# Pooled attention into a Gelu MLP: values of attention two slots later, and the remainder's query loads split three and five

## The chip, the cores and the metric

The kernel runs on one core of a Trainium2 chip, in one launch. The metric is device time in microseconds (us). Before the change the median of seven runs is 279.15 us (278.59 to 280.13).

Five engines share the work: TensorE (PE, with its weight loads PEld), VectorE (DVE), ScalarE (ACT), GpSimd (POOL) and SyncE (SP, which here only issues DMAs). Sixteen DMA engines move data for all of them.

## The reference

Attention with keys and values that are averaged over eight neighbours, and then an MLP on its output:

```python
B, H, S, D = 8, 8, 576, 64
k_p = k.reshape(B, H, S // 8, 8, D).mean(axis=3)
v_p = v.reshape(B, H, S // 8, 8, D).mean(axis=3)
attn = softmax(q @ k_p.T / sqrt(D))          # 576 x 72 for each batch and head
x = (attn @ v_p).transpose(0, 2, 1, 3).reshape(4608, 512)
out = gelu_tanh(x @ w_in) @ w_out            # w_in 512 x 2048, w_out 2048 x 512
```

Inputs and output are float32; the kernel's matmuls take bf16.

## The kernel before, in words

**Tiling.** The 4608 rows are worked off in nine blocks of 512. Blocks 0 to 7 are the first 512 rows of each batch. The remaining 64 rows of all eight batches make the ninth block, R. The order is `seq` = 0, 1, ..., 6, R, 7. A step is one turn of the loop at L826; it is numbered here by its place in `seq`, so step 7 works on R. Each step has the MLP of its own block and, woven into it, the attention of the next block. In step 2, and from step 3 on in a `fast` form, this is so:

- The hidden layer, `hidden_fast` (L462): products of 128x256 tiles (L474) that save a multiplication in eight by sums and differences made on VectorE (`x_sums`, L448, recorded at L458), and ordinary products (L383). The partial results lie in two PSUM tiles, `x4` and `y4`. ScalarE and VectorE empty them in turn: L500, L502, L507, L510, L513, L517. ScalarE applies Gelu.
- The output layer in `mlp` (L536): seven products of 16 matmuls (L586), also with sums and differences.
- The attention of the next block: pooling on VectorE (L149, L151, L152, L165), transpose of the pooled keys by a DMA (L211, into `kTd`), their spread into `kbd` on GpSimd (L218, recorded at L94), spread of values on GpSimd (L172), scores (L248), exponentials (L257), sums and normalization (L264, L273, L279), transpose of the weights by four DMAs (L306, into `eT`), and the values (`values`, L326; matmuls at L344, for R at L355), whose result is copied to `xT` by three copies on ScalarE and one on VectorE (L361, recorded at L92 and L94). `xT` is what the next step's first products read.

**Order.** The order on each engine is written out by hand. TensorE's matmuls of a step have slot numbers: 0 to 63 for the hidden layer, 64 to 175 for the output layer (64 + 16 n + 8 p + m for product n, half p and matmul m). `at(hooks, s, f, ...)` (L771) puts the instructions of `f` ahead of the matmul of slot s on whatever engine they run. So the scores stand at slots 68 and 90, and the values at 64 + 104 (L892): between the two halves of the last product, with eight matmuls behind them before the next step begins. Step 1 splits the values in two, at 64 + 100 and 64 + 107 (L889, L890).

**Loads.** Loads and stores of blocks are issued by SP, those of R's queries by GpSimd. They are eight transfers of 128 KB, one for each batch (L125), which fill one tile `q_sb`. They are issued at slot 9 of the steps that lie three and two places ahead of R in the order: four in step 4 (batches 0 to 3) and four in step 5 (batches 4 to 7), in the loop at L896. Ahead of each group a tiny copy on GpSimd (`gate_queries`, L196) waits for L502 of the same step, so that the transfers don't start earlier. `load_q` takes a half-open range of columns, two batches to a column.

Of the kernel before, what the change touches and what calls it, by code (L numbers as in the profile page):

```python
# [19 lines left out]
def kernel(  # L20
# [21 lines left out]
    nc = tc.nc  # L42
    B, H, S, D = q.shape
# [9 lines left out]
    R = B  # L53
# [63 lines left out]
    def load_q(g, j0, j1, eng):  # L117
        t = st[g]["q"]
        if g < B:
            src = q[g, :, :MAIN, :].rearrange("h (p j) d -> p h j d", j=4)  # L120
            eng.dma_start(out=t[:, :, j0:j1], in_=src[:, :, j0:j1])
        else:
            for b in range(2 * j0, 2 * j1):
                p0 = 64 * (b % 2)
                eng.dma_start(out=t[p0:p0 + 64, :, b // 2, :], in_=q[b, :, MAIN:, :].rearrange("h t d -> t h d"))  # L125

# [518 lines left out]
    load_half(0, "k", nc.sync)  # L645
    load_half(0, "v", nc.sync)
    load_q(0, 0, 2, nc.sync)
    load_main(0, "v", 0, 2, nc.sync)
    load_main(0, "v", 2, 4, nc.sync)
    load_q(0, 2, 4, nc.sync)  # L650
    nc.scalar.preload_act_table_set(EXP_SET)

# [99 lines left out]
    load_half(1, "k", nc.sync)  # L752
    load_half(1, "v", nc.sync)
    load_q(1, 0, 4, nc.sync)
    for c in range(4):
        w_out_load(c)
# [14 lines left out]
    def at(hooks, s, f, *a):  # L771
        hooks.setdefault(s, []).append(lambda: f(*a))
# [6 lines left out]
    hooks = {}  # L779
# [46 lines left out]
    for n_, g in enumerate(seq):  # L826
        if n_ == 0:
            continue
        hooks = {}
        fast = n_ >= 3  # L830
        if n_ == 1:
            for i in range(1, 4):
                at(hooks, i, w_sums, i, 0, NP, nc.vector)
            at(hooks, 36, g_sums, 0, 4)
            at(hooks, 57, g_sums, 4, 6, (0,))
        elif fast:
            at(hooks, 41, g_sums, 0, 2, (0,))
            at(hooks, 57, g_sums, 2, 6, (0,))
            at(hooks, 65, g_sums, 6, 8, (0,))
            at(hooks, 65, g_sums, 0, 4, (1,))  # L840
        else:
            at(hooks, 20, g_sums, 0, 2)
            at(hooks, 36, g_sums, 2, 4)
            at(hooks, 57, g_sums, 4, 6, (0,))
        if not fast:
            at(hooks, 65, g_sums, 6, 8, (0,))
        at(hooks, 64 + 32, g_sums, 4, 8, (1,))
        if n_ + 1 < len(seq):
            n = seq[n_ + 1]
            b = B - 1 if n == R else n  # L850
            kv = n != B - 1
            if n_ == 1:
                for j in range(4):
                    at(hooks, 22 + 4 * j, cast_q, n, j, j + 1, nc.scalar)
                at(hooks, 35, qT_tile, n)
                at(hooks, 35, q_transpose_dma, n)
            if kv and not fast:
                t0 = 22 if n_ == 1 else 12
                at(hooks, t0, pool, b, 0, 5)
                at(hooks, t0, dup_k, b, 0, 5)  # L860
                at(hooks, t0, kT_tile, b, None)
                at(hooks, t0, k_transpose_dma, b)
                t1 = t0 + (16 if n_ == 1 else 24)
                at(hooks, t1, pool, b, 5, 9)
                at(hooks, t1, k_spread, b, [nc.gpsimd, nc.gpsimd])
                at(hooks, t1, spread_v, b, nc.gpsimd)
            elif kv:
                at(hooks, 5, pool, b, 0, 5, (0,))
                at(hooks, 17, pool, b, 0, 5, (1,))
                at(hooks, 17, dup_k, b, 0, 5)  # L870
                at(hooks, 17, kT_tile, b, None)
                at(hooks, 17, k_transpose_dma, b)
                at(hooks, 17, spread_gated, b)
                at(hooks, 40, k_spread, b, [nc.gpsimd, nc.gpsimd])
            if fast:
                at(hooks, 2, qT_tile, n)
                at(hooks, 2, q_transpose_dma, n)
            sc_at = [68, 68, 90, 90]
            for j in range(4):
                at(hooks, sc_at[j], scores, n, j)  # L880
                at(hooks, sc_at[j] + 1, exps, n, j)
            at(hooks, 80, eT_tile, n)
            for j in range(4):
                at(hooks, 80 if j < 2 else 92, norm, n, j, nc.vector if j > 1 else nc.gpsimd)
                at(hooks, 80 if j < 2 else 92, e_transpose_dma, n, j)
            at(hooks, 64 + 66, nc.scalar.preload_act_table_set, GELU_SET)
            at(hooks, 64 + 100, xT_tile, n)
            if n_ == 1:
                at(hooks, 64 + 100, values, n, (0,))  # L889
                at(hooks, 64 + 107, values, n, (1,))  # L890
            else:
                at(hooks, 64 + 104, values, n)  # L892
        if n_ + 2 < len(seq):
            n2 = seq[n_ + 2]
            s2 = 44 if n_ == 1 else 57
            for half, ahead in enumerate((3, 2)):  # L896
                if n_ + ahead < len(seq) and seq[n_ + ahead] == R:
                    if half == 0:
                        at(hooks, 9, q_tile, R)
                    at(hooks, 9, gate_queries, g)  # L900
                    at(hooks, 9, load_q, R, 2 * half, 2 * half + 2, nc.gpsimd)
            if n2 != R:
                at(hooks, s2, q_tile, n2)
                at(hooks, s2, load_q, n2, 0, 4, nc.sync)
            at(hooks, 64 + 52, cast_gated, n2)
            if n_ < 2:
                at(hooks, 64 + 100, qT_tile, n2)
                at(hooks, 64 + 100, q_transpose_dma, n2)
                at(hooks, 64 + 100, load_kv, n2, (1,))
            elif n2 != B - 1:  # L910
                b2 = B - 1 if n2 == R else n2
                at(hooks, 64 + 84, pool, b2, 5, 9, (0,))
                at(hooks, 64 + 97, pool, b2, 5, 9, (1,))
            if n_ == 1:
                at(hooks, 45, load_kv, n2, (0,))
            else:
                at(hooks, 28, load_kv, n2)
        mlp(g, hooks, n_ + 1 == len(seq), fast)
# [30 lines left out]
```

## Time and profile before

| What | us |
|---|---|
| median of 7 runs | 279.15 |
| lowest and highest | 278.59, 280.13 |
| the profiled execution | 279.03 |
| its span in the profile | 277.1 |
| TensorE busy | 269.1 (97%) |
| VectorE busy | 222.6 (80%) |
| ScalarE busy | 176.2 (64%) |
| GpSimd busy | 81.8 (30%) |
| bytes moved by DMA | 54.37 MB, 196 GB/s in the mean |

Times in the lines of a profile are counted from the start of the span. A line of a timeline has the start, the length, the engine, the line of the kernel, the operation with its tiles, and in brackets the idle time of the engine before it with what ended it. `x16` counts instructions. TensorE's granted clock is at full speed in all forty slices of the page. Landing of a DMA is counted from the start of its issue. "SPq" and "POOLq" are the queues of SP and GpSimd.

### The profile page before, as it was taken

The page shows a single profiled execution, that of the slowest core. Times are in us where ns is not written, and L with a number is a line of the kernel's source. Part 1 is how long each engine was busy: PE and PEld are TensorE (multiplying, and loading weights), DVE is VectorE, ACT ScalarE, POOL GpSimd, SP SyncE. Part 2 cuts the span into 40 slices and gives each one's busy share as a digit, 9 for nine tenths or more (in the row PEclk, how much of TensorE's full clock was granted, in tenths as well). Part 3 has the DMA queues.
Part 4 walks back from the last instruction along what each step waited for, and adds up shares of the span by engine and source line. Part 5 has one row for each costly group of instructions (what it writes and reads, how often), then busy time and mean ns, then how long its engine had stood idle before and what let it go on. Part 6 is the DMA issues. An engine that isn't in the chain of part 4 may idle for free.

```text
span 277.1 us, 6558 instructions
## 1 busy us (share of the span) xinstructions
PE 269.1 (97%) x2668; PEld 192.5 (69%) x2686; DVE 222.6 (80%) x365; ACT 176.2 (64%) x265; POOL 81.8 (30%) x122
## 2 busy tenths in 40 slices
PE   8989999999999999999999999999999999999995
PEld 3668844446854587668866876688668966886684
DVE  5887769999966798989999979899989558956832
ACT  1586576488546764696469636964796469656820
POOL 4740272006420544314264445433223300300000
PEclk9999999999999999999999999999999999999999
DMA  7999999998989895799399988974842460243013
GB/s 235 308 192 287 368 386 223 301 359 217 255 201 242 254 282 142 176 307 246 115 223 283 266 147 205 237 202 125 174 155 47 125 151 2 50 103 98 1 41 114
DMA packets 67856, 54.37 MB, mean 196 GB/s; under 512 B 41458, under 2 KB 53746, under 8 KB 67826
## 3 DMA queue, kind: packets, MB, share of 16 engines
q1 hardware_dynamic: 65186, 50.67, 70.2%
q0 software_dynamic: 2496, 3.15, 6.4%
q8 instruction: 21, 0.34, 0.5%
q10 hardware_dynamic: 144, 0.13, 0.1%
q14 instruction: 9, 0.07, 0.1%
HBM read 36.70 MB, written 9.44 MB: 166 GB/s over the span
## 4 chain that ended last, share of the span: by engine, by line
PE 85%; DVE 7%; DMA 4%; issue 1%; SPq 1%; ACT 1%; DVEq 0%
PE mm L586 28%; PE mm L383 22%; PE c L474 13%; PE mm L399 5%; PE mm L394 5%; PE xo L344 3%; PE x L586 3%; DMA eT<-eb 2%; DMA q_sb<-in_q_dram 2%; PE sc L248 2%; DVE den L264 1%; PE mm L531 1%; DVE eb L279 1%; ACT gT L490 1%; DVE eb L291 1%
## 5 line engine op out<-in xcount | busy, mean ns | idle before, releaser
L383 PE MATMUL mm<-xT,w_in_b 128*128 128x512 bf16 x290 | 68.1, 379 | 0.7
L586 PEld LDWEIGHTS <-gT 128*128 128x128 bf16 x512 | 48.3, 98 | 9.0 <-issue 1.4
L385 ACT ACTIVATE gT<-mm 128x512 bf16<-128x512 f32 x76 | 43.5, 599 | 15.3 <-PE mm L383 15.0
L383 PEld LDWEIGHTS <-w_in_b 128*128 128x128 bf16 x304 | 29.7, 98 | 30.8
L586 PEld LDWEIGHTS <-stage 128*128 128x128 bf16 x384 | 37.5, 98 | 4.4
L92 ACT CAST xT<-xo 128x512 bf16<-128x512 f32 (+1 forms) x24 | 13.2, 610 | 29.9 <-PE xo L344 25.4
L586 PE MATMUL mm<-tw,gT 128*128 128x256 bf16 x240 | 30.0, 273 | 0.0
L586 PE MATMUL mm<-w_out_b,gT 128*128 128x256 bf16 x240 | 29.9, 273 | 0.0
L279 POOL TENSOR_TENSOR eb<-e,r 128x576 bf16<-128x576 f32 x14 | 15.8, 1149 | 45.5 <-DVE r L273 24.8
L264 DVE TENSOR_REDUCE den<-e 128x8 f32<-128x576 f32 x36 | 26.2, 728 | 2.8 <-ACT e L257 2.8
L257 ACT ACTIVATE e<-sc 128x576 f32<-128x576 f32 x36 | 22.5, 650 | 7.8 <-POOL eb L279 5.9
L586 PE MATMUL mm<-tw,stage 128*128 128x256 bf16 x224 | 26.7, 273 | 0.0
L92 ACT COPY osb<-mm 128x512 f32<-128x512 f32 x30 | 17.8, 593 | 13.8 <-PE mm L586 13.2
L149 DVE TENSOR_TENSOR kv<-kv 128x1024 f32<-128x1024 f32 (+3 forms) x19 | 22.2, 1166 | 3.0 <-DMA kv<-in_k_dram 1.8
L172 POOL TENSOR_TENSOR vbd<-kvb,vmask 128x256 bf16<-128x256 bf16 (+2 forms) x38 | 21.8, 595 | 7.3 <-DVE kvb L152 6.4
L94 POOL CAST q_b<-q_sb 128x1024 bf16<-128x1024 f32 (+1 forms) x15 | 17.6, 1191 | 20.1 <-DMA q_sb<-in_q_dram 20.1
L474 PEld LDWEIGHTS <-ws 128*128 128x128 bf16 x192 | 18.8, 98 | 6.1 <-issue 0.2
L279 DVE TENSOR_TENSOR eb<-e,r 128x576 bf16<-128x576 f32 x18 | 17.8, 987 | 0.6
L474 PE MATMUL c<-tt,ws 128*128 128x256 bf16 x144 | 17.7, 272 | 0.0
L434 DVE TENSOR_TENSOR stage<-gT 128x512 bf16<-128x512 bf16 (+1 forms) x25 | 13.5, 541 | 4.2 <-ACT gT L385 2.3
L94 POOL COPY kbd<-kTd 64x288 bf16<-64x288 bf16 x12 | 6.5, 544 | 34.7 <-DMA kTd<-kvb 34.3
L435 DVE TENSOR_TENSOR gT<-gT 128x512 bf16<-128x512 bf16 (+1 forms) x25 | 13.2, 528 | 3.4 <-ACT gT L385 1.2
(107 smaller groups left out, 424.5 us busy)
## 6 DMA issues: line engine op xcount, KB each, us to landing
kv<-in_k_dram SPq DMA_DIRECT2D x7, 1024.0 KB, 7.3
q_sb<-in_q_dram SPq DMA_DIRECT2D x7, 1024.0 KB, 9.8
kv<-in_v_dram SPq DMA_DIRECT2D x6, 1024.0 KB, 9.4
out_dram<-osb SPq DMA_DIRECT2D x12, 512.0 KB, 3.0
out_dram<-osb SPq DMA_DIRECT2D x11, 256.0 KB, 3.3
kv<-in_v_dram SPq DMA_DIRECT2D x4, 512.0 KB, 10.1
w_in_b<-in_moe_w_in_dram POOLq DMA_DIRECT2D x4, 512.0 KB, 6.7
w_out_s<-in_moe_w_out_dram SPq DMA_DIRECT2D x2, 1024.0 KB, 13.7
```

Of the source, the lines that this page charges most:

```text
L92: eng.copy(out=out, in_=in_)
L94: eng.tensor_copy(out=out, in_=in_)
L149: add(out=t[:, :, 0:4, :], in0=t[:, :, 0:4, :], in1=t[:, :, 4:8, :], op=ALU.add)
L172: eng.tensor_tensor(out=vbd[p0:128, b, n0:n1, :].rearrange("p (c r) (hh d) -> p c (r hh) d", c=max(m, 1), d=D), in0=kvb[p0:128, 4 + c0:4 + ...
L257: nc.scalar.activation(out=e.rearrange("p (x h) s -> p x (h s)", x=2), in_=sc[:, :, 0:4 * Sp], func=ACT.Exp, scale=1.0 / 64.0)
L264: nc.vector.reduce_sum(out=den, in_=e, axis=AX.X)
L279: eng.tensor_tensor(out=o.rearrange("p (pr hh s) -> p hh pr s", hh=2, s=Sp), in0=e.rearrange("p (hh pr) s -> p hh pr s", hh=2), in1=r.rear ...
L383: nc.tensor.matmul(out=hp, lhsT=w_in_b[:, ko, fo * 128:(fo + 1) * 128], rhs=st[g]["xT"][:, ko, :], start=(i == 0), stop=(i == KO - 1))
L385: nc.scalar.activation(out=gT[:, fo, :], in_=hp, func=ACT.Gelu_apprx_tanh)
L394: nc.tensor.matmul(out=hp[:, f, :], lhsT=w_in_b[:, ko, (fo + f) * 128:(fo + f + 1) * 128], rhs=st[g]["xT"][:, ko, c0:c0 + 256], start=(ko ...
L474: nc.tensor.matmul(out=acc[:, m, :], lhsT=lhs(i, m), rhs=rhs(i), start=bool(fresh and i == 0 and m % 2 == 0), stop=(i == 1), skip_group_ch ...
L586: nc.tensor.matmul(out=xs[p] if acc is xs else acc[:, p, :], lhsT=lt, rhs=rt, start=bool(fresh and m == 0 and (p == 0 or (last and acc is ...
```

## The change

In steps 2 to 7 the values stand two slots later, at 64 + 106, so that six matmuls of the last product lie behind them and two more ahead. `load_q` for R takes a range of batches now, and the loop gives it batches 0 to 2 in step 4 and batches 3 to 7 in step 5. No instruction is added or removed.

```diff
-            for b in range(2 * j0, 2 * j1):
+            for b in range(j0, j1):
                 p0 = 64 * (b % 2)
                 eng.dma_start(out=t[p0:p0 + 64, :, b // 2, :], in_=q[b, :, MAIN:, :].rearrange("h t d -> t h d"))
...
             else:
-                at(hooks, 64 + 104, values, n)
+                at(hooks, 64 + 106, values, n)
...
-            for half, ahead in enumerate((3, 2)):
+            for ahead, b0, b1 in ((3, 0, 3), (2, 3, B)):
                 if n_ + ahead < len(seq) and seq[n_ + ahead] == R:
-                    if half == 0:
+                    if b0 == 0:
                         at(hooks, 9, q_tile, R)
                     at(hooks, 9, gate_queries, g)
-                    at(hooks, 9, load_q, R, 2 * half, 2 * half + 2, nc.gpsimd)
+                    at(hooks, 9, load_q, R, b0, b1, nc.gpsimd)
```

## The prediction

> Steps are numbered by their place in `seq`: step 2 works on batch 2, step 7 on the remainder R, step 8 is the last. A boundary is the stretch from the values of the next step (L344, L355) to its first product (L474).
>
> **What bounds the kernel now.** I read the page first, then the chain of waits, then the timelines of single engines at the places that the chain names, last the DMA queues there.
>
> ```profile
> PE 269.1 (97%) x2668; PEld 192.5 (69%) x2686; DVE 222.6 (80%) x365; ACT 176.2 (64%) x265; POOL 81.8 (30%) x122
> ```
>
> TensorE is busy for 97% of the span; only a place where it stands still can gain or lose time. The stretches from first product to first product (steps 3, 4, 5, 7) show how much stands still:
>
> ```profile
> 109.04:136.60 27.56, 27.45 (x297) 20.70 (x297) 25.28 (x40) 19.11 (x29) 8.27 (x13) 1.00 0.76 203
> 136.60:165.01 28.41, 27.66 (x296) 20.64 (x296) 25.57 (x41) 19.09 (x29) 13.05 (x18) 1.00 0.99 233
> 165.01:192.66 27.65, 27.54 (x296) 20.85 (x296) 25.49 (x40) 19.10 (x29) 11.69 (x18) 1.00 0.75 182
> 220.86:248.30 27.44, 27.34 (x296) 20.71 (x296) 20.11 (x34) 18.50 (x27) 2.26 (x2) 1.00 0.31 68
> ```
>
> The first number after the stretch is its length, the last but one the share of time in which the DMA engines work. Step 4 is 0.85 us longer than step 3 and its DMA engines never rest (0.99). The chain tells where the time lies (start, length, what):
>
> ```profile
> 104.58 2.63 DMA eT<-eb
> ...
> 107.26 0.97 PE xo L344 x24
> ...
> 117.03 1.85 PE c L474 x16
> ...
> 144.58 1.86 PE c L474 x16
> ...
> 159.21 3.98 DMA eT<-eb
> ...
> 163.22 0.97 PE xo L344 x24
> ...
> 173.00 1.84 PE c L474 x16
> ...
> 178.72 0.49 PE sc L248 x32
> ...
> 200.65 1.85 PE c L474 x16
> ...
> 228.84 1.75 PE c L474 x16
> ```
>
> Three kinds of stop. (a) The values wait for the fourth transpose of the weights (eT) in steps 2 and 4. In TensorE's timeline of step 4:
>
> ```profile
> 162.18 0.41 PE L344 MATMUL xo<-eT,vbd 32*64 32x256 bf16 x8
> 163.22 0.97 PE L344 MATMUL xo<-eT,vbd 32*64 32x256 bf16 x24 [0.64 <-DMA eT<-eb]
> ```
>
> The values run from 162.18 to 164.20, 2.02 us, against 1.19 us in step 3: 0.83 us lost. In step 2 they take 1.46 us: 0.27 us lost.
>
> (b) The last two products of the hidden layer (16 matmuls, L474) take 1.84 to 1.86 us in steps 3 to 6 and 1.75 us in steps 7 and 8. The 0.10 us is a wait for VectorE: the second of the two writes into the bank that L513 reads. VectorE in step 5:
>
> ```profile
> 165.63 0.42 DVE L458 TENSOR_TENSOR tt<-xT 128x512 bf16<-128x512 bf16 x1 [0.66 <-ACT xT L92]
> ...
> 171.18 1.21 DVE L510 COPY stage<-c 128x1024 f32<-128x1024 f32 x1
> 172.53 1.22 DVE L513 TENSOR_TENSOR stage<-c,stage 128x1024 f32<-128x1024 f32 x1
> ```
>
> From 165.63, when ScalarE's third copy of xT lets it start, VectorE has eleven instructions without a gap (the left-out lines have no bracket), L513 ends at 173.75, and the product starts at 173.80. So in steps 3 to 6 this chain of VectorE, which starts with the values, is the bound up to here. In step 7 there is no pooling in it and it waits for TensorE.
>
> (c) In step 5 the scores (0.49 us instead of 0.38) wait for the spread of k on GpSimd, which waits for the transpose of k:
>
> ```profile
> 177.46 1.25 POOL L94 COPY kbd<-kTd 64x288 bf16<-64x288 bf16 x2 [2.23 <-DMA kTd<-kvb]
> ```
>
> 177.46 + 1.25 = 178.71, and the second half of the scores starts at 178.76. Nothing is in hand there: R's queries are loaded just ahead of it.
>
> **The change part by part.**
>
> **Values two slots later**, in steps 2 to 7. No instruction is added. Eight matmuls after the values take 0.88 us (164.13 to 165.01), so two slots are 0.22 us. Before the values TensorE has 0.22 us more to do, after them six matmuls (0.66 us) instead of eight.
> - At a boundary that waits for eT (steps 2, 4) up to 0.22 us of the wait is filled and the next step's products start 0.22 us earlier.
> - At the others (3, 5, 6, 7) the values, the three copies of xT on ScalarE, the copy of x behind them (L611) and VectorE's chain come 0.22 us later, the first product does not. The first copy was done at 164.61 for a product at 165.01: 0.40 us in hand, 0.18 after; no wait. L611 frees the bank of hidden(0): it ended at 166.09 for a matmul at 166.76, still 0.45 in hand. But VectorE's chain has nothing in hand in steps 3 to 6: the product behind L513 comes 0.22 us later relative to the first product, whichever boundary lies before. That is 4 x 0.22 = 0.88 us, if nothing absorbs it. In steps 7 and 8 the product at 229.55 has 0.26 us over L513's end (229.29) and the chain there starts from TensorE: nothing.
>
> **Queries of R: three in step 4, five in step 5.** Eight issues of 0.71 us on GpSimd as before (L125), one of them in another step. In step 4 GpSimd is 0.71 us earlier with vbd; in step 5 it is 0.71 us later: vbd ended at 175.23 and the next, the spread of k, waited 2.23 us for its DMA, so this is hidden; without that cover it would cost the scores 0.71 us. SP's queue has no step moved past; but its loads queue behind the same engines.
>
> What one transfer costs the DMA engines, in step 5 (168.5 to 178.5), and then single microseconds from 174 and from 175:
>
> ```profile
> q0 software_dynamic: 192, 0.52, 25.3%
> ```
> ```profile
> q0 software_dynamic: 3, 0.01, 8.1%
> ```
> ```profile
> q0 software_dynamic: 47, 0.13, 81.7%
> ```
>
> 25.3% of 10 us is 2.53 us for four: 0.63 us each; in step 4 (140 to 150) the share is 21.2%, 0.53 us each.
> - Step 4: the engines are full from the loads to the transposes; the load of the next queries, issued at 147.31, lands 12.1 us later at 159.4, and the fourth eT, queued behind, at 163.18. One transfer less takes 0.53 us off; the loads are issued 0.22 us later, as VectorE's chain is. Estimate: 163.18 - 0.53 + 0.22 = 162.9. The bounds are 162.0 (issue at 159.4 and the 2.6 us of the uncrowded steps) and 163.4 (nothing gained).
> - Step 5: does the fifth transfer hold up the transpose of k? It was issued at 171.29 and landed 6.1 us later, against 2.6 us in steps 3 and 6, where no R is loaded. From below zero: a transfer ahead of it can't make it land earlier, so no gain. From above: all of 0.63 us. The row for the fourth transfer speaks for the low end: issued at 171.70, it has 3 packets on the engines in 174 to 175 and its 47 only in 175 to 176, when k's transpose is through; it landed after 5.5 us. A fifth, issued 0.7 us behind it, would follow. The Trainium skill speaks for the high end: "DMA: Bandwidth & Descriptors", section on queues, rings and completion order, says that each engine goes round-robin between the queues at packet level, so that what is issued on GpSimd takes turns with the transpose. By the row the cost is 0, by the rule up to 0.63. The two completions at 177.17 and 177.40 lie so close that I can't exclude some delay; I take 0.3 us, the middle.
>
> **The sum**, as shift of TensorE against before:
> - boundary 2: -0.22; behind L513 in step 3: +0.22, so 0.
> - behind L513 in step 4: +0.22.
> - boundary 4: the half that waits is now due at 162.59 + 0.22 + 0.22 = 163.03, eT lands at 162.9: no wait. Values end at 162.18 + 0.44 + 1.19 = 163.81 against 164.20, and the step starts 0.22 earlier still: -0.60.
> - behind L513 in step 5: +0.22, so -0.38; scores in step 5: +0.3, so -0.08.
> - behind L513 in step 6: +0.22. Total +0.14 us.
>
> The profiled execution took 279.03 us (span 277.1 and 1.9 around it), so 279.17; the median of the seven runs is 0.12 above it: 279.15 + 0.14 = 279.3.
>
> **The rivals.**
> 1. Slower: the fifth transfer holds up k's transpose in step 5 by its whole 0.63 us or more, the place with nothing in hand. For it: k's transpose lost 3.5 us (6.1 against 2.6) behind four transfers, 0.88 each; with 0.88 in place of 0.3 the sum is +0.72: 279.9. It decides from a delay of 0.72 us (sum +0.56) on. Against it: the order of the packets. Chance 0.22.
> 2. Slower by step 4: eT does not land earlier, because one engine of sixteen lags and not the sum of bytes. For it: the first two eT of step 4 landed 5.0 and 5.8 us after issue, and between 174 and 175 in step 5 the engines moved 25 GB/s while a transpose hung. eT at 163.4 instead of 162.9 puts 0.37 us plus 0.2 for the restart back (before, 0.64 us of waiting cost 0.83): +0.7, 279.85. Chance 0.13.
> 3. Faster: VectorE's chain gives way (a gap that the profile doesn't show, or TensorE catching up in a later wait), so the three lags in steps 4 to 6 are not paid. Then -0.22 - 0.83 + 0.3 = -0.75: 278.4. For it: both stops of kind (a) are what the edits touch; against it: the 0.10 us wait of kind (b) is in all four steps. Chance 0.15.
> The likeliest case, +0.14 with 0 to 0.63 us for the disputed term, has 0.50: 279.0 to 279.5.
>
> **How the numbers follow.** A measurement can tell about 0.2% from no change, 0.56 us: 278.6 to 279.7. Likeliest case: within. Rivals 1 and 2: slower. Rival 3: faster. So 0.15, 0.50, 0.35. The range takes in rival 3 to just above its value and rival 1 with some margin, leaving 0.2 out: 278.5 to 280.2.
>
> **What would show it.** Right: in the chain the eT entry at step 4's end is gone or under 0.2 us; the 16 matmuls of L474 take about 2.07 us in steps 3 to 6 and 1.75 in 7 and 8; step 5's spread of k starts up to 0.6 us later against its first product than before (12.45 us). Wrong: L474 at 1.85 (VectorE not the bound), the scores of step 5 beyond 1 us (rival 1), or an eT wait of 0.6 us still at step 4 (rival 2).

## The result, and the profile after

The kernel is slower. Its median is 280.32 us (14 runs, 279.75 to 282.27) against 279.12 us for the kernel before, run beside it (36 runs): 1.20 us between the medians. Some runs of a kernel fall in a slower state, and the ratios here and below are estimated without those, so that they differ a little from the quotient of the medians. This one is 1.0048, with a 95% interval of 1.0035 to 1.0061, or 1.34 us more, where 0.14 us had been forecast. The profiled execution took 280.91 us, with a span of 279.0 us.

TensorE's share of the span on the page is that of before, so again only the places count where it stands still:

```profile
PE 269.4 (97%) x2668; PEld 192.5 (69%) x2686; DVE 222.2 (80%) x365; ACT 176.0 (63%) x265; POOL 79.7 (29%) x122
```

The stretches of steps 3, 4, 5 and 8 of the kernel after follow (length; busy time of PE, PEld, DVE, ACT and POOL with their instructions; granted clock, share of busy DMA engines, GB/s):

```profile
109.50:137.40 27.90, 27.51 (x296) 20.71 (x296) 25.44 (x41) 18.93 (x28) 8.28 (x13) 1.00 0.78 208
137.40:165.46 28.06, 27.71 (x296) 20.59 (x296) 25.71 (x41) 19.09 (x28) 10.98 (x17) 1.00 0.97 225
165.46:194.03 28.57, 27.73 (x297) 20.81 (x297) 25.14 (x41) 19.11 (x28) 12.94 (x19) 1.00 0.79 196
...
249.89:279.00 29.11, 25.51 (x200) 19.47 (x199) 14.87 (x25) 13.87 (x23) 0.00 (x0) 1.00 0.23 69
```

Step 4 is 0.35 us shorter than before, and steps 3, 5 and 8 are longer by 0.34, 0.92 and 0.32 us (step 8 took 28.79 before). The clock is 1.00 everywhere. The chain of waits of the same kernel names what stands at these places:

```profile
145.13 1.24 DVE stage L513
146.41 1.03 PE c L474 x8
...
159.88 3.96 DMA eT<-eb
163.89 0.97 PE xo L344 x24
...
171.96 6.59 DMA kTd<-kvb
...
178.61 0.64 POOL kbd L94
...
180.13 0.45 PE sc L248 x30
...
255.33 1.01 ACT osb L507
256.38 1.03 PE c L474 x8
```

L513 is in the chain now by itself: the product behind it starts 0.04 us after it ends. In step 4 eT is still there. In step 5 the transpose of k (kTd) and its spread are new. In step 8 a copy of ScalarE is new, L507. Its wait shows in ScalarE's timeline, first before, then after; the last bracket is the idle time and what ended it:

```profile
253.42 1.01 ACT L507 COPY osb<-c 128x1024 f32<-128x1024 f32 x1 [0.84 <-DMA out_dram<-osb]
```
```profile
255.32 1.01 ACT L507 COPY osb<-c 128x1024 f32<-128x1024 f32 x1 [1.15 <-PE c L474]
```

L507 starts 5.11 us into step 8 before and 5.43 after. The second bracket names TensorE, but that product was done about 0.8 us earlier. What came last is the landing of an output store, 5.33 us into the step, which frees the buffer that L507 writes. SP issues the two halves of this store (L419) here, before and after:

```profile
249.41 1.25 SPq L419 DMA_DIRECT2D out_dram<-osb  x2
```
```profile
251.21 1.25 SPq L419 DMA_DIRECT2D out_dram<-osb  x2
```

One execution carries chance as well. Step 3 starts 0.46 us later in the profile after, but the last matmul of step 1's values is 0.74 us late there already, mostly by a wait for qT in step 1, which the change doesn't touch. So I profiled both kernels a second time and compare means of two. The first piece runs from that last matmul of step 1's values to the first product of step 3. The forecast is put into the same pieces. Lengths in this table are from the instructions' own times, and can differ by 0.02 us from those of the rounded stretches above.

| us | before, two profiles | after, two profiles | difference | forecast |
|---|---|---|---|---|
| boundary 2 and what leads to it | 29.46, 29.36 | 29.18, 29.21 | -0.22 | -0.22 |
| step 3 | 27.55, 27.55 | 27.90, 27.77 | +0.28 | +0.22 |
| step 4 | 28.42, 28.57 | 28.06, 29.01 | +0.04 | -0.60 |
| step 5 | 27.65, 27.63 | 28.57, 28.57 | +0.93 | +0.52 |
| step 6 | 28.19, 28.19 | 28.41, 28.41 | +0.22 | +0.22 |
| step 7 | 27.45, 27.45 | 27.45, 27.45 | 0 | 0 |
| step 8 | 28.79, 28.82 | 29.13, 29.03 | +0.27 | 0 |
| sum | | | +1.52 | +0.14 |

1.52 us agrees with the 1.34 of the ratio (0.98 to 1.70 by the interval). Steps 4, 5 and 8 hold nearly all of the miss: 0.64 + 0.41 + 0.27 = 1.32 us.

### The profile page after: what moved, and what is told of

Read it like the earlier page. It is cut to its first block, busy times and chain, and to the rows that moved or that the text cites. A ratio compares the mean times of both kernels' runs of the same rounds, so it can differ in the third digit from the quotient of the medians.

```text
span 279.0 us, 6558 instructions
## 1 busy us (share of the span) xinstructions
PE 269.4 (97%) x2668; PEld 192.5 (69%) x2686; DVE 222.2 (80%) x365; ACT 176.0 (63%) x265; POOL 79.7 (29%) x122
## 4 chain that ended last, share of the span: by engine, by line
PE 79%; DVE 10%; DMA 8%; issue 1%; SPq 1%; ACT 1%; POOL 1%; DVEq 0%; ACTq 0%
PE mm L586 32%; PE mm L383 16%; PE c L474 9%; PE mm L399 5%; PE mm L394 5%; PE xo L344 3%; PE x L586 3%; DMA kTd<-kvb 2%; PE sc L248 2%; DMA q_sb<-in_q_dram 2%; DMA qT<-q_b 2%; DVE kv L149 1%; DMA eT<-eb 1%; PE mm L531 1%; DVE osb L502 1%; DVE kv L151 1%
## 5 line engine op out<-in xcount | busy, mean ns | idle before, releaser
L383 PEld LDWEIGHTS <-w_in_b 128*128 128x128 bf16 x304 | 29.7, 98 | 30.8
L264 DVE TENSOR_REDUCE den<-e 128x8 f32<-128x576 f32 x36 | 26.3, 730 | 3.4 <-ACT e L257 3.4
L92 ACT COPY osb<-mm 128x512 f32<-128x512 f32 x30 | 17.8, 593 | 14.5 <-PE mm L586 13.7
L172 POOL TENSOR_TENSOR vbd<-kvb,vmask 128x256 bf16<-128x256 bf16 (+2 forms) x38 | 22.4, 610 | 7.3 <-DVE kvb L152 6.4
L474 PEld LDWEIGHTS <-ws 128*128 128x128 bf16 x192 | 18.8, 98 | 6.9 <-issue 1.1
L94 POOL CAST q_b<-q_sb 128x1024 bf16<-128x1024 f32 (+1 forms) x15 | 15.5, 1053 | 19.9 <-DMA q_sb<-in_q_dram 19.9
L474 PE MATMUL c<-tt,ws 128*128 128x256 bf16 x144 | 17.7, 272 | 0.5 <-ACT osb L507 0.5
L279 DVE TENSOR_TENSOR eb<-e,r 128x576 bf16<-128x576 f32 x18 | 17.2, 958 | 0.6
L474 PEld LDWEIGHTS <-w_in_b 128*128 128x128 bf16 x144 | 14.1, 98 | 2.6 <-issue 1.0
```

What stands on the lines that cost most here:

```text
L92: eng.copy(out=out, in_=in_)
L94: eng.tensor_copy(out=out, in_=in_)
L172: eng.tensor_tensor(out=vbd[p0:128, b, n0:n1, :].rearrange("p (c r) (hh d) -> p c (r hh) d", c=max(m, 1), d=D), in0=kvb[p0:128, 4 + c0:4 + ...
L264: nc.vector.reduce_sum(out=den, in_=e, axis=AX.X)
L279: eng.tensor_tensor(out=o.rearrange("p (pr hh s) -> p hh pr s", hh=2, s=Sp), in0=e.rearrange("p (hh pr) s -> p hh pr s", hh=2), in1=r.rear ...
L383: nc.tensor.matmul(out=hp, lhsT=w_in_b[:, ko, fo * 128:(fo + 1) * 128], rhs=st[g]["xT"][:, ko, :], start=(i == 0), stop=(i == KO - 1))
```

## The experiments

My theory going in: what is lost is VectorE's lag behind L513, the fifth transfer ahead of k's transpose in step 5, and the store ahead of L507 in step 8. The first rival: the later values alone do it, and the queries play no part. The second: step 4's relief never came. The expectations speak of the theories as they stood when each run was made. A ratio below is to the kernel before on the same chip, with its 95% interval; step lengths are from one profile each.

**Each edit alone, twice.** Values only is the kernel before with one line changed:

```diff
-                at(hooks, 64 + 104, values, n)
+                at(hooks, 64 + 106, values, n)
```

> Only the values two slots later; the queries of R stay four and four. Theory A (three separate lags: VectorE's chain to L513, the store behind L507, the transpose of k in step 5): boundary 2 gives -0.22 us, step 3 takes +0.22 to +0.35, steps 4, 5 and 6 +0.22 each behind L513, the eT wait of step 4 stays and swallows 0.22, step 8 takes +0.33 at L507: +0.8 us in sum. Theory B (the loss is the fifth transfer alone): -0.2 to +0.2 us. In the profile by A: step 8's 29.1 us instead of 28.8, steps 3 and 6 0.2 us longer, scores of step 5 no later than 0.3 us against their first product.

> Values at 64 + 106, queries four and four. Steps 3 and 6 +0.22 each, step 4 +0.2 to 0.4, step 5 +0.3 to 1.4 (the scores already had nothing in hand), step 8 +0.3: +1.3 to 2.5 us by the first trace, +0.6 by the first timing. Above +1.2 us the values alone carry the loss; under +0.6 they carry half at most.

Measured: 1.0021 (1.0003 to 1.0039) and 1.0052 (1.0031 to 1.0072). Step 5 of these two profiles:

```profile
165.62:194.65 29.03, 27.79 (x296) 20.91 (x296) 24.75 (x41) 19.01 (x28) 11.86 (x18) 1.00 0.84 182
```
```profile
165.47:193.39 27.92, 27.77 (x298) 20.80 (x296) 25.61 (x41) 19.00 (x28) 11.96 (x18) 1.00 0.76 187
```

The first expectation had 0.22 us for step 5; it is 1.38 and 0.27 over before, with four transfers ahead of k's transpose as before. So the fifth transfer is not the only way to lengthen this step. Queries only is the kernel after with that line put back:

> Only the queries three and five; the values stay at 64 + 104. Theory A: step 4 about 0.4 us shorter since eT lands earlier, step 5 0.7 us longer since the transpose of k lands and is spread later; sum +0.3 us, steps 3, 6, 7, 8 as before. Theory B: +1.2 us, all of it in step 5.

> Queries three and five, values at 64 + 104. By the sum of the traces: step 4 0.5 us shorter than before, step 5 0.75 longer: +0.25 us, ratio 1.001. If the fifth transfer is the whole loss: 1.004.

Measured: 0.9993 (0.9969 to 1.0016) and 0.9998 (0.9984 to 1.0013). So the values alone cost 0.2 to 0.5%, from nearly half of the loss to all of it, and the queries alone make no difference that the runs can tell. But that zero is a sum of two. The stretches of steps 4 and 5 with the queries only, second profile:

```profile
137.03:164.60 27.57, 27.57 (x299) 20.64 (x297) 25.59 (x41) 19.11 (x29) 11.08 (x17) 1.00 0.96 226
164.60:192.94 28.34, 27.76 (x298) 20.80 (x296) 25.39 (x41) 19.21 (x29) 13.01 (x19) 1.00 0.79 200
```

Step 4 has lost its stop (27.57; PE busy all of it), and step 5 has a new one of 0.7 us. The first profile shows 27.98 and 28.40.

**The kernel after, and before, again,** as controls:

> The changed kernel once more, beside the three others on one chip: ratio 1.0035 to 1.0061 as measured first. In the profile the fixed parts must come again: last product of the hidden layer at 9.01 us of steps 4, 5 and 6, step 8 0.3 us longer than before. What comes out otherwise (the waits for eT in step 4, for qT in step 1, for the store in step 3) varies from one execution to the next.

> The kernel before once more, for a second profile of it: ratio 1.000. Fixed parts as in its first profile (last product of the hidden layer at 8.79 us of steps 3 to 6; steps 3 and 6 at 27.55 and 28.19 us). Open is how far step 4 (28.42) and step 5 (27.65) vary by themselves: if step 5 comes out at 28.4 or more here too, the five transfers are not what cost it.

Measured: 1.0051 (1.0024 to 1.0077) and 1.0003 (0.9988 to 1.0018). What matters is step 4 of the kernel after, second profile:

```profile
137.29:166.29 29.00, 27.87 (x298) 20.65 (x296) 26.04 (x41) 19.07 (x28) 11.95 (x17) 1.00 1.01 224
```

29.00 us, with the same code that took 28.06 in the first: -0.43 and +0.52 us against the mean of before. The fourth eT landed 26.44 us into the step there and 27.39 here. In the two runs below that share this step's code (the swap, and the fifth transfer behind the spread) it took 28.23 and 28.11. So there is some relief in three profiles of four and none in the fourth; the mean of the four is 0.14 us under before, not 0.04 over it.

**The store behind L507.** The hidden layer's k0 gets the spare buffer, and k1, which is written later, the buffer that the store reads:

```diff
-        k2, k0, k1 = part(), part(), spare
+        k2, k1, k0 = part(), part(), spare
```

> The changed kernel, with the buffers of k0 and k1 exchanged: k0, which L507 writes at 4.6 us of a step, gets the spare tile, and k1, which L510 writes at 6.2 us, the output tile whose store is still under way. If the store behind L507 is one of the lags: step 8 back from 29.1 to 28.8 us or less, step 3 from 27.9 to 27.8, no stop of TensorE at the product behind L507; about 0.4 us under the changed kernel, ratio to before 1.003 instead of 1.0048. If L507 is only where a lag shows that has another cause, the time stays at 1.0048.

> Values at 64 + 106, queries four and four, k0 and k1 exchanged, so that L507 waits for no store: 0.3 to 0.4 us under values alone; step 8 at 28.75 us. If the store behind L507 costs nothing: the same as values alone.

Measured: 1.0015 (0.9998 to 1.0032) on the kernel after, 1.0039 (1.0013 to 1.0064) on values only. Step 8 is 28.75 us in both, against 29.02 to 29.27 in the six profiles with values at 106 and without the swap; L507 starts at 4.55 us of it. So the store is the whole of step 8's loss, and a little more (28.79 before). The store's landing has some chance in it: with the values at 104 and no swap, step 8 is 28.78 to 28.90 us in six profiles and 29.02 and 29.05 in two.

**VectorE's chain behind L513.** The second part of the pooling, the duplication and transpose of k and the spread of values moved from slot 17 to slot 33 in steps 3 and 6, behind L513:

```diff
-                at(hooks, 17, pool, b, 0, 5, (1,))
+                t0 = 33 if n_ in (3, 6) else 17
+                at(hooks, t0, pool, b, 0, 5, (1,))
...
-                at(hooks, 17, k_transpose_dma, b)
+                at(hooks, t0, k_transpose_dma, b)
```

> The changed kernel with the second pooling stage, the copy of k, its transpose and the spread of values moved from slot 17 to slot 33 in steps 3 and 6 alone: three instructions of VectorE, 1.6 us, go behind L513. Theory A (VectorE's chain to L513 is the bound): the last product of the hidden layer starts at 8.69 us of steps 3 and 6 instead of 9.01, while it stays at 9.01 in steps 4 and 5; steps 3 and 6 up to 0.3 us shorter, unless the transpose of k, now issued near 10 us, keeps the scores waiting (due at 13.6). Rival (the product waits for something else that comes with the values, such as ScalarE's copies): 9.01 stays in steps 3 and 6 too.

Measured: 1.0244 (1.0204 to 1.0284). TensorE's timeline of step 3, which starts at 109.06 us here:

```profile
117.75 1.04 PE L474 MATMUL c<-tt,w_in_b 128*128 128x256 bf16 x8
...
125.77 0.22 PE L248 MATMUL sc<-kbd,qT 64*64 64x72 bf16 x2 [3.09 <-POOL kbd L94]
```

The product behind L513 starts at 8.69 us of the step, as in steps 7 and 8, instead of 9.01 in the kernel after and 8.79 before. In step 6 it starts at 8.76, and in steps 4 and 5, where nothing was moved, at 9.01. That confirms the lag. The move costs more than it saves: k's transpose, issued at 10.0 us, lands at 15.98, and the scores wait 3 us (step 3: 32.84 us; step 6: 29.07).

**The slot as a dose.** Four kernels have the swap and few queries ahead of k's transpose, so that steps 3 and 4 have no other stop; the values stand at 103, 104, 106 and 108. At 104, 106 and 108 the queries are one in step 4, three in step 5 and four behind the spread of k; at 103 two, three and three:

```diff
-            for ahead, b0, b1 in ((3, 0, 3), (2, 3, B)):
+            for ahead, b0, b1 in ((3, 0, 1), (2, 1, 4)):
...
+            if n2 == R:
+                at(hooks, 41, load_q, R, 4, B, nc.gpsimd)
```

> Values one slot earlier than before the change, at 64 + 103; k0 and k1 exchanged; queries of R two in step 4, three at slot 9 and three at slot 41 of step 5. Theory A: the 0.10 us stop behind L513 goes in steps 3 to 6 (last product at 8.69), -0.4 us; against it eT of steps 4 and 5 is due 0.11 us earlier. Ratio 0.995 to 0.997. Rival (eT is the bound at the boundaries): waits of 0.2 us or more for eT in steps 4 and 5, no gain over 0.997.

> The kernel before with k0 and k1 exchanged and the queries of R issued by GpSimd as one in step 4, three at slot 9 of step 5 and four at slot 41 of step 5, behind the spread of k; values at 64 + 104. Theory A: eT of step 4 lands near 25.6 us of the step instead of 26.6, so its wait goes (-0.8); the scores of step 5 don't wait (-0.1); step 8 doesn't wait at L507 (-0.1); sum -1.0 us, ratio 0.9964. Rival (the transfers only crowd another stretch): eT of step 5 lands behind 25.8 us of its step and gives back up to 1 us.

> The split one, three, four with k0 and k1 exchanged, in which neither eT in step 4 nor the transpose of k in step 5 nor a store keeps TensorE waiting, with the values at 64 + 106 instead of 64 + 104. Theory A (each slot later lags VectorE's chain by 0.11 us in steps 3 to 6): last product of the hidden layer at 9.01 us instead of 8.79 in the four steps, 0.9 us over the same kernel with 104, ratio near 1.000. Rival (the values' place costs nothing by itself): 0.997 as with 104.

> As the clean kernel with 106, but the values four slots later than before the change, at 64 + 108. Theory A, twice the dose: last product at 9.2 us of steps 3 to 6, measured from a first product that now waits for ScalarE's first copy too (four matmuls, 0.44 us, before it, and a copy of 0.59), 1.8 to 2.1 us over the kernel with 104: ratio 1.0035 to 1.0045. Rival: less than 1 us.

| values at | step 3 | step 4 | step 5 | step 6 | step 7 | step 8 | ratio |
|---|---|---|---|---|---|---|---|
| 103 | 27.46 | 27.49 | 27.91 | 28.09 | 27.45 | 28.74 | 0.9962 (0.9949 to 0.9975) |
| 104 | 27.55 | 27.55 | 27.84 | 28.19 | 27.45 | 28.76 | 0.9971 (0.9960 to 0.9983) |
| 106 | 27.77 | 27.77 | 27.82 | 28.41 | 27.45 | 28.75 | 0.9995 (0.9981 to 1.0008) |
| 108 | 27.99 | 27.99 | 27.99 | 28.54 | 27.54 | 28.72 | 1.0032 (1.0018 to 1.0045) |

Each slot costs 0.10 to 0.11 us in steps 3, 4 and 6 (0.06 in step 4 from 103 to 104, 0.07 in step 6 beyond 106), and nothing in step 7 up to 106. (In step 5 the versions at 103 and 104 wait for eT, behind the late queries, and values that stand later fill this wait.) From 104 to 106 that is 0.63 us over the steps, and 0.67 us by the ratios (0.0024 x 279.1; the kernel with 104 ran on another chip than the other three). The versions at 103 and 104 beat both kernels; the best has a median of 278.32 us beside 279.11.

**The fifth transfer in step 5.** In the kernel after I put the fifth behind the spread of k:

```diff
-            for ahead, b0, b1 in ((3, 0, 3), (2, 3, B)):
+            for ahead, b0, b1 in ((3, 0, 3), (2, 3, 7)):
...
+            if n2 == R:
+                at(hooks, 41, load_q, R, 7, B, nc.gpsimd)
```

> The changed kernel with the fifth transfer of step 5 issued at slot 41, behind the spread of k, so that four transfers lie ahead of it as before the change. Theory A: in the traces with five transfers the last packet of k's transpose left at the same time as with four (10.5 us of the step), and only its landing came 0.7 us later, with the fifth transfer's packets in between; so the landing goes back from 13.1 to about 12.6 us of the step (12.4 and the 0.2 of the later issue), the stop of the scores from 0.8 us to 0.1, and the time to about 0.7 us under the changed kernel: ratio to before 1.002. Rival (the page of instructions that TensorE fetches holds up k's transpose, whatever the transfers): landing at 13.1 or later as before, no gain.

Measured: 1.0034 (1.0014 to 1.0054), and step 5 is 29.03 us, longer than the kernel after: with only four ahead kTd landed 14.00 us into the step, later than with five (13.10). That is what the rival said, and by itself it speaks against the theory; the time lies 0.47 us under the kernel after on the same chip (1.0051), within the noise. So the same with the values back at 104, twice:

> Values at 64 + 104; queries three in step 4, four at slot 9 of step 5 and the last at slot 41, behind the spread of k. If the fifth transfer's price is the 0.75 us in the scores of step 5: 0.75 us under queries three and five, landing of k's transpose at 12.0 to 12.4 us of step 5, ratio 0.998. If k's transpose is held up by something else (with the values at 106 the same edit left the landing at 14.0): no difference to three and five.

> Queries three, four and one behind the spread once more. If four ahead give the landing of before (11.9 to 12.4 us of step 5): step 5 at 27.65, ratio 0.997. If step 5 comes out at 28.3 again: the number of transfers ahead of k's transpose does not decide.

Measured: 0.9992 (0.9973 to 1.0011) and 0.9994 (0.9978 to 1.0011); step 5 took 28.35 in the first profile and 27.55 in the second. A ratio of 0.997 to 0.998 was expected; against queries three and five on the same chip (0.9998) the first is 0.17 us faster, less than the runs can tell. And four in step 4 with five in step 5 at 104; one batch is loaded twice, with the same data:

```diff
-            for ahead, b0, b1 in ((3, 0, 3), (2, 3, B)):
+            for ahead, b0, b1 in ((3, 0, 4), (2, 3, B)):
```

> Values at 64 + 104; four transfers in step 4 as before and five at slot 9 of step 5, batch 3 loaded twice with the same data. If the fifth transfer ahead of k's transpose costs step 5 its 0.7 us: landing near 13.0 us of step 5, step 5 at 28.3, step 4 at 28.4 to 28.6 as before, +0.7 us, ratio 1.0025. If the relief of step 4 moves the stop into step 5: step 5 stays at 27.65, ratio 1.000.

Measured: 1.0020 (1.0004 to 1.0035), 28.31 and 28.35 us in steps 4 and 5. That is the kernel before with one transfer added: +0.56 us over 22 runs (0.11 to 0.98).

Why do two profiles of one kernel (queries three, four and one) differ by 0.8 us in step 5? SP's queue shows a difference. The issue of k's transpose in the second profile, then in the first with the issue behind it, a load of the next k:

```profile
170.97 2.32 SPq L211 DMA_TRANSPOSE kTd<-kvb  x1
```
```profile
170.17 1.20 SPq L211 DMA_TRANSPOSE kTd<-kvb  x1
171.43 1.74 SPq L112 DMA_DIRECT2D kv<-in_k_dram  x1
```

The issue takes either 1.9 to 2.7 us or 1.20 us. After a short one SP starts to issue the load of the next k 0.7 to 1.5 us earlier in the step (for the same slot of the values), but one of the two issues of k behind it then takes 1.2 to 1.8 us instead of 0.5 to 0.6. The queue that the views call `instruction` goes with this. It moves one packet of 16 KB in step 5. From 171.5 to 171.7 us, in the second and then in the first profile (packets, MB, share of the engines):

```profile
q8 instruction: 1, 0.02, 42.5%
```
```profile
q8 instruction: 1, 0.02, 40.2%
```

So it starts under the transpose's issue in the second profile and under the load's in the first. In all twenty profiles it starts 6.75 to 7.15 us into step 5 where the transpose's issue is long (nine), and at 7.42 to 8.02 where it is short (eleven). Sorted by the length of the issue, kTd's landing in step 5 (us into the step, and the step's length in brackets):

| transfers ahead | long issue | short issue |
|---|---|---|
| 3 | 11.16 (27.84) | 11.08 (27.91), 11.61 (27.82), 11.92 (27.99) |
| 4 | 11.71 (27.55), 11.94 (27.63), 12.39 (27.65) | 12.67 (27.93), 12.99 (28.35), 13.36 (28.62), 13.89 (29.03), 14.00 (29.03) |
| 5 | 12.62 (28.35), 12.81 (28.57), 13.10 (28.57), 13.14 (28.40) | 12.79 (28.35), 13.62 (29.03), 13.72 (29.04) |

The first column is in order: every landing with five is later than every one with four. The packet of instructions doesn't make this order, since it starts at 6.91 to 7.15 us in all seven of them. At 104 the step is 0.77 us longer in the mean (28.38 against 27.61). Both profiles of the kernel after lie in this column too; they are 0.93 longer than before, and 0.22 of that is L513's. But no profile with the values at 106 and four ahead has a long issue, so at 106 this column has nothing to compare them with.

In the second column the order is gone: four ahead land at 12.67 to 14.00, five at 12.79 to 13.72. At 104 the short issue goes with a landing about 1 us later with four ahead, and with no difference with three or five (a profile each; the one with three stands at 103). It is in all three profiles with the values only and in the one with the fifth behind the spread, which is why they cannot speak for or against the fifth transfer. With the values at 106 or 108 it came in eight of ten profiles; at 103 or 104 in three of ten. What sets the time of the packet of instructions no run shows, so the rival named with the fifth transfer behind the spread, that the instructions' page holds up the transpose, stays open for the short issues.

So this is what stands on the fifth transfer: the profiles with a long issue show 0.77 us for it at 104; the times of the runs show 0.17 to 0.56, and only the last, with one transfer added, is clear of the noise. That the fifth makes step 5 of the kernel after longer is argued from there. The sorting was made after the profiles had been seen.

**All queries late, on SP.** From the kernel before, without transfers in step 4 and with all eight behind the loads in step 5:

```diff
-                    at(hooks, 9, load_q, R, 2 * half, 2 * half + 2, nc.gpsimd)
...
+                if n2 == R:
+                    at(hooks, 28, q_tile, R)
+                    at(hooks, 28, load_q, R, 0, B, nc.sync)
```

> The kernel before, with all eight transfers of R's queries issued by SP in step 5 behind the loads of keys and values, none by GpSimd. If crowding by these transfers causes both the eT wait of step 4 and the zero slack of the scores in step 5: the eT wait is gone (-0.8 us), the transpose of k in step 5 lands 2.6 us after its issue, sum -0.9 us. If the crowding of step 4 is made by the other loads alone, the eT wait stays and the sum is -0.1. If the transfers now crowd the end of step 5, eT of step 5 lands late: 0 to +1 us.

Measured: 1.0066 (1.0043 to 1.0090). Step 4's stop is gone (27.55) and kTd of step 5 lands at 9.34 us, 3.05 us after its issue (in the profiled execution, which at 280.17 us is the fastest of its runs). But SP's issues and the engines' work then hold up eT of step 5, which lands at 27.68 instead of 25.05, and the step takes 29.51. So the queries are what delays kTd, and all of them behind it cost more than the stops that they remove: 1.85 us by the ratio, more than the 0 to 1 us that the expectation allowed.

## Why the prediction was wrong

**Boundary 2, -0.22: right.** It is -0.22 between the two pairs. Over nine profiles with the values at 106 and nine at 104 it is smaller, -0.13, because eT waits at this boundary in only some of them.

**VectorE behind L513, +0.22 in each of steps 3 to 6: right.** The dose gives 0.22 in steps 3, 4 and 6, and 0 in step 7; moving the pooling off the chain takes it away. The prediction's sign of it, 16 matmuls of L474 at about 2.07 us, shows in the chain as a group of eight that is split off behind L513.

**Boundary 4, forecast at -0.60 for the step, measured +0.04 (-0.14 over four profiles): the term that failed most.** The step that failed is the estimate of the fourth eT at 162.9 us, 26.3 into the step: 0.53 us off for one transfer, 0.22 on for the later loads. The landings of the fourth eT, in us into step 4:

| transfers in step 4 | values at 104 | values at 106 | difference of the means |
|---|---|---|---|
| four | 26.48, 26.59, 26.74 | 26.68, 27.09, 27.26 | +0.41 |
| three | 25.70, 25.74, 25.80, 26.15 | 26.44, 26.50, 26.61, 27.04, 27.39 | +0.95 |
| gain of one less | 0.76 | 0.21 | |

At 104 one transfer less gives more than the 0.53 taken. At 106 it gives 0.21 in the mean, less than the scatter of the landings (the 27.04 is from the run with the pooling moved in step 3). So the two terms of the estimate don't add: the later loads cost 0.41 us with four transfers and 0.95 with three, where 0.22 was taken. The loads are late already on the way: with three transfers in both, the first load of the next k lands at 14.5 to 15.7 us at 104, and at 15.6 to 16.7 at 106. One profile of the kernel after comes near the forecast (-0.43), and the other has the outcome of rival 2 (+0.52); its reason, one engine of sixteen that lags, was not tested. Why loads that are issued 0.22 us later land up to 1 us later stays open.

**Scores of step 5, forecast at +0.3, measured +0.71 (0.93 less L513's 0.22): the size was wrong.** It was the outcome of rival 1, with its decision point of 0.72 nearly met. The mechanism, the fifth transfer ahead of k's transpose, is shown at 104 as far as said above; the values alone lengthen this step too, by 0.27 and 1.38 us in two profiles. Two things stand behind the size in the profiles with a long issue.

First, the prediction weighed the row of packets (0) against the rule of taking turns (0.63). The last packet of kTd's data starts at 10.10 to 10.57 us into the step with three, four and five transfers (10.52, 10.49 and 10.57 in the profiles that landed at 11.16, 12.39 and 13.14), so the row was read rightly for the data. What is late is the completion. Behind the data the trace has 32 packets of 4 bytes; the last of them starts at 10.54 us with three, 10.49 to 10.98 with four and 11.20 to 11.77 with five, and the landing follows 0.6, 1.2 to 1.4, and 1.4 us behind it. The Trainium skill states in "DMA: Bandwidth & Descriptors", section "Queues, rings and completion order", that the increment of the semaphore lands only after every earlier write of that engine, across its queues. That fits these numbers; no run here separates it from other reasons for a late completion. With a short issue the last data packet is late as well, by up to 1.2 us (10.40 to 11.70).

Second, the landing doesn't reach the scores one to one. The spread of k in GpSimd's timeline and VectorE's timeline beside it, both with the queries only, and then the spread with four ahead:

```profile
177.28 1.72 POOL L94 COPY kbd<-kTd 64x288 bf16<-64x288 bf16 x2 [1.61 <-DMA kTd<-kvb]
```
```profile
177.19 0.69 DVE L435 TENSOR_TENSOR gT<-gT 128x1024 bf16<-128x1024 bf16 x1
177.91 0.80 DVE L436 TENSOR_TENSOR stage<-gT 128x1024 bf16<-128x1024 bf16 x1
```
```profile
176.45 1.25 POOL L94 COPY kbd<-kTd 64x288 bf16<-64x288 bf16 x2 [1.54 <-DMA kTd<-kvb]
```

Alone the two copies take 0.90 us (steps 3 and 6 before the change); here they take 1.72 and 1.25. Beside VectorE's sums of 0.69 us one copy grows from 0.42 to 0.72 or even 0.88 us, and the sum to 0.80. The Trainium skill's page "SBUF — State Buffer", section "Who interferes with whom", has a reason that fits, though no run here tests it: a VectorE instruction with two inputs in SBUF and a GpSimd instruction that reads SBUF need one port, and the first to come keeps it. So with the values at 104 the spread ends at 13.70 us for landings of 11.94 and 12.39, and at 14.40 to 14.45 for landings from 12.62 to 13.14: a delay of 0.2 to 1.2 us turns into one of 0.70.

**Step 8, forecast at 0, measured +0.27, and the 0.06 to 0.13 in step 3: overlooked.** The prediction followed L611 to the bank that it frees and found 0.45 us in hand. It didn't follow it to the store. The store is issued 0.21 us later (1.95 instead of 1.74 us into step 8), lands 3.3 to 3.4 us on, and L507 must wait for it before it writes the same buffer. The row was there: before the change, L507's bracket already names out_dram. In step 3 the landing of 5.37 us is late enough to show in one profile (step 3 at 27.90) and stays under L513's lag in the other (5.23; 27.77).

## What to carry to other kernels

A step that is moved later is followed to all that it releases: an output copy sets a store, the store's landing frees a buffer, and a copy that waits for it already has nothing in hand. Ahead of a DMA that is on the critical chain, count the transfers of every queue that are outstanding, since its completion can be late when its data is not. Gains at a stop that depends on crowded DMA engines are to be taken from several profiles: one execution showed -0.43 us, the next +0.52.

## What the runs showed of the hardware

- Transfers of 128 KB on GpSimd's queue, in flight ahead of a transpose on SP's queue, make its landing later. With long issues it is 3.05 us from issue to landing with none ahead, 4.9 with three, 5.4 to 6.1 with four, 6.3 to 6.9 with five. From three to five its last data packet stays at 10.1 to 10.6 us of the step (8.7 with none).
- SP's issue of the same transpose takes 1.20 us or 1.9 to 2.7 us in executions of the same kernel. It is long where a packet of 16 KB on the `instruction` queue starts 6.75 to 7.15 us into the step, and short where it starts at 7.42 to 8.02; then a load's issue behind it is long. With four transfers ahead the short one goes with a later landing (12.7 to 14.0 against 11.7 to 12.4 us). These are correlations.
- A copy on GpSimd of 0.42 us takes 0.72 to 0.97 us beside sums on VectorE, and these grow from 0.69 to as much as 0.88 us.
- An output store of 1.25 us of issue lands 3.2 to 3.5 us after its second half is issued (with the buffers as before), in the tail where the DMA engines are busy 0.24 of the time.
